# A token-major convolution on TensorE: from two 70x64 tiles of 192 columns to eight 39x32 tiles of 96 columns

## The chip, the cores and the metric

The kernel runs on one core of one Trainium2 chip. The metric is the device time of one execution in microseconds (us). Every ratio is between runs on the same chip in the same batch; traces are also compared across batches. Ratios use runs in the fast state alone; three runs, two of `start_after` and one of `best`, were more than 1.5% above the fastest of their kernel and are left out of them. The profile of a kernel is taken from one execution and shows a span some 1.8 us shorter than the time of the run.

Engines are named as the profile names them: PE is TensorE's matmuls, PEld its weight loads, DVE is VectorE, ACT ScalarE, POOL GpSimd, SP SyncE. L301 is line 301 of the kernel profiled, so the same statement has another number in another kernel.

## The reference, cut to what matters

```
# x: 8 x 4160 x 192 float32, weight: 8 heads x 7 taps
w   = softmax(weight, axis=-1)
y   = causal 7-tap convolution of x along the sequence, one set of taps per head of 24 channels
x2  = y.reshape(33280, 192)
h   = max(max(x2 @ w1, x2 @ w2), x2 @ w3)        # 192 -> 768
out = h @ w_out                                  # 768 -> 192, float32
```

## The kernel before

The 33280 tokens are worked on in 65 blocks of 512. The maximum is rewritten: max(y w1, y w2, y w3) = max(relu(y(w1-w3)), y(w2-w3)) + y w3, and the last term goes straight to the output through a small product M = w3 w_out. So per block TensorE does six groups of **layer one** (tiles `lp` and `lq`, one per half of the 128 rows, six matmuls of 512 columns in a group) and 60 matmuls of the **second layer** (tile `po`, 192 columns, in two halves of 30).

Layer one wants the convolved y with channels on partitions. Blocks 0 to 3 get it from a dense convolution (tile `D`). From block 4 on the convolution is token-major: x is loaded with tokens on partitions, GpSimd casts it to 16 bit, TensorE multiplies it by a band matrix of the taps (tile `G`), ScalarE and VectorE bring G to SBUF (tile `ys`), a DMA transposes it to channels on partitions, and two more DMAs **swap** the halves of the rows, so that each channel is there in both. Block 4 is done alone; blocks 5 and 6, 7 and 8, and so on in pairs, one convolution per pair: 30 pairs.

```
    def cast_x(t):                                   # GpSimd, 2 casts per block
        ...
        K = HALF + PAD                               # 64 + 6 rows
        for c in range(2):
            nc.gpsimd.tensor_copy(out=x16s[t0][0:K, :, c, u, :, :].rearrange("p h r c -> p r h c"),
                                  in_=xf[0:K, c:NR:2, :].rearrange("p r (h c) -> p r h c", c=GRP))
    ...
    def conv(t, pools):                              # 16 matmuls, 192 columns for a pair
        ...
        for h in range(NHEAD):
            for c in range(2):
                nc.tensor.matmul(
                    G[h // per][HALF * c:HALF * (c + 1), h % per, :],
                    lhsT=band[0:HALF + PAD, h, PAD:HALF + PAD],
                    rhs=x16s[t0][0:HALF + PAD, h, c, :, :, :].rearrange("p u r c -> p (u r c)"),
                    start=True, stop=True, tile_position=(0, HALF * c))
    ...
    def l1(t, j, pools=((psp, "p"), (psq, "q"))):    # one group of layer one
        ...
        for c in range(NC):
            for i in range(2):
                row = slice(HALF * i, HALF * (i + 1))
                nc.tensor.matmul(ps[i][:, 0:N], lhsT=wd[row, c, P * j:P * (j + 1)], rhs=y_all(t, i, c),
                                 start=(c == 0), stop=(c == NC - 1))
        r = rp.tile([P, NBLK], FP16, tag="r", name=f"r_{t}_{j}")
        nc.scalar.activation(out=r[:, 0:N], in_=ps[0][:, 0:N], func=AF.Relu)
        nc.vector.tensor_max(out=hs[t][:, j, 0:N], in0=r[:, 0:N], in1=ps[1][:, 0:N])
    ...
    for t in range(2, NB):                           # the main loop, cut
        ...                                          # loads of x, swaps, casts
        l1(t, 0)
        u = convs_at.get(t, t + 3 if t % 2 == 0 else NB)
        conv(u, PQ if t == 2 else WW + PQ)           # takes p and q buffers of layer one too
        ...                                          # evacuation of G, transposes
        st2(t - 1, 0, NJ)
        for j in range(1, NJ):
            l1(t, j)
            st2(t - 1, j, NJ)
        ...
```

The softmax here doesn't subtract the row's maximum and nothing guards it: scores larger than these inputs give would overflow.

## Time and profile before

| kernel before | |
|---|---|
| time, median of the runs with the changed kernel | 467.44 us (467.29 to 467.9) |
| span of the profile | 466.3 us |
| PE busy | 99% |
| one pair of blocks, from convolution to convolution | 13.74 us |
| of it TensorE held by the convolution | 0.87 us |
| last matmul starts | 462.39 us |

The prediction below shows the page of this profile: engines, chain and timeline. What it does not show is how close the two engines behind layer one are. These two lines are from the costliest groups: line, engine, operation, output and input, shapes, count, then busy time and the mean ns of one, then the idle time before it and what ended that.

```profile
L404 DVE TENSOR_TENSOR h<-r,lq 128x512 f16<-128x512 f16 x386 | 264.5, 685 | 98.6 <-ACT r L403 98.6
L403 ACT ACTIVATE r<-lp 128x512 f16<-128x512 f32 x386 | 230.5, 597 | 137.4 <-PE lp L399 123.9
```

A group of layer one is released only after ScalarE's 0.60 us and then VectorE's 0.69 us. There are two `q` buffers, so while that runs, TensorE must have other work. TensorE's timeline behind a convolution shows how it comes out; the columns are the start, the length and the piece of work.

```profile
209.34 0.38 PE L399 MATMUL lp<-yd,wd 64*128 64x512 f16 x1
209.44 0.37 PE L399 MATMUL lq<-yd,wd 64*128 64x512 f16 x1
209.55 0.38 PE L399 MATMUL lp<-yd,wd 64*128 64x512 f16 x1
```

`lq` starts 0.10 us behind `lp` and so keeps the beat of 0.21 us between two matmuls of one half. There is next to no room left in this place, and I did not see that when I predicted.

### The profile page before, as it was taken

How to read it: one execution, taken by the hardware profiler on the slowest of the kernel's cores; microseconds unless marked ns; L12 is line 12 of the kernel's file. 1: busy time of each engine (PE TensorE's matmuls, PEld its weight loads, DVE VectorE, ACT ScalarE, POOL GpSimd, SP SyncE). 2: the span in 40 equal slices, each digit the busy share in tenths (PEclk: the TensorE clock that was granted, in tenths of full speed). 3: DMA queues.
4: the chain of work that ended last, by engine and by line, in shares of the span. 5: the costliest groups of instructions: out<-in, count | busy, mean ns of one | idle time of the engine just before them, and what ended most of it. 6: DMA issues, size and time to landing. Idle time of an engine off the chain costs nothing.

```text
span 466.3 us, 17191 instructions
## 1 busy us (share of the span) xinstructions
PE 460.1 (99%) x7065; PEld 385.6 (83%) x7065; DVE 359.6 (77%) x607; ACT 317.0 (68%) x609; POOL 162.7 (35%) x227
## 2 busy tenths in 40 slices
PE   8899999999999999999999999999999999999996
PEld 4587888888888888889888888988888898888996
DVE  6787777777777777787877777777778777787775
ACT  5766767667666676676766667676676666766664
POOL 5664334234324324423423432432442343243010
PEclk9999999999999999999999999999999999999999
DMA  8958997778687777878777768767686976784512
GB/s 201 238 119 198 208 232 174 171 198 172 170 202 191 149 188 174 180 175 204 178 152 197 170 181 189 181 157 200 177 176 165 210 178 153 190 166 108 118 69 103
DMA packets 107114, 81.14 MB, mean 174 GB/s; under 512 B 53110, under 2 KB 101980, under 8 KB 107036
## 3 DMA queue, kind: packets, MB, share of 16 engines
q1 hardware_dynamic: 99804, 55.17, 57.6%
q0 software_dynamic: 7072, 24.78, 14.8%
q8 instruction: 55, 0.90, 0.9%
q14 instruction: 23, 0.19, 0.1%
q10 hardware_dynamic: 160, 0.10, 0.1%
HBM read 30.28 MB, written 25.56 MB: 120 GB/s over the span
## 4 chain that ended last, share of the span: by engine, by line
PE 95%; DMA 2%; SPq 2%; POOL 0%; issue 0%; DVE 0%; ACT 0%
PE lq L399 34%; PE po L442 33%; PE lp L399 22%; PE G L301 5%; DMA wos<-in_moe_w_out_dram 2%; SPq L190 1%; PE D L319 0%; SPq L134 0%; POOL wo L515 0%; PE pm L280 0%; PE pm L284 0%; DVE o L452 0%; ACT a L451 0%
## 5 line engine op out<-in xcount | busy, mean ns | idle before, releaser
L404 DVE TENSOR_TENSOR h<-r,lq 128x512 f16<-128x512 f16 x386 | 264.5, 685 | 98.6 <-ACT r L403 98.6
L403 ACT ACTIVATE r<-lp 128x512 f16<-128x512 f32 x386 | 230.5, 597 | 137.4 <-PE lp L399 123.9
L399 PE MATMUL lp<-yd,wd 64*128 64x512 f16 x1158 | 311.9, 376 | 1.3 <-DVE wd L256 1.3
L399 PE MATMUL lq<-yd,wd 64*128 64x512 f16 x1158 | 312.0, 376 | 0.0
L442 PE MATMUL po<-wo,h 64*128 64x192 f16 x3120 | 248.9, 243 | 0.0
L442 PEld LDWEIGHTS <-h 64*128 64x128 f16 x3120 | 203.6, 94 | 17.4
L399 PEld LDWEIGHTS <-wd 64*128 64x128 f16 x2340 | 166.6, 94 | 28.0 <-issue 3.4
L471 POOL DMA_DIRECT2D out_dram<-o x64 | 48.1, 752 | 281.4 <-DVE o L452 215.0
L158 POOL CAST x<-xf 70x768 f16<-70x768 f32 x122 | 97.4, 833 | 3.0 <-DMA xf<-in_x_dram 2.6
L442 PE MATMUL po<-m,yd 64*128 64x192 f16 x780 | 95.7, 243 | 0.0
L452 DVE TENSOR_TENSOR o<-a,po 128x384 f32<-128x384 f32 (+1 forms) x132 | 71.3, 542 | 0.6 <-ACT a L451 0.6
L442 PEld LDWEIGHTS <-yd 64*128 64x128 f16 x780 | 57.8, 94 | 10.8
L451 ACT COPY a<-po 128x384 f32<-128x384 f32 (+1 forms) x132 | 62.0, 471 | 2.1 <-PE po L442 2.1
L347 DVE CAST ys<-G 128x384 f16<-128x384 f32 x61 | 31.0, 550 | 0.0
L301 PEld LDWEIGHTS <-band 70*64 70x64 f16 x496 | 19.5, 109 | 12.8 <-PE lp L399 12.7
L347 ACT CAST ys<-G 128x384 f16<-128x384 f32 x61 | 26.2, 485 | 0.0
L301 PE MATMUL G<-x,band 70*64 70x192 f16 (+1 forms) x496 | 26.1, 248 | 0.0
L215 PE MATMUL idle<-idle 128*128 128x512 f16 x15 | 6.5, 581 | 1.2 <-DVE idle L210 1.2
L177 POOL CAST xz<-xf 112x80 f16<-112x80 f32 (+2 forms) x18 | 5.4, 340 | 3.9 <-DMA xf<-in_x_dram 3.0
L319 PEld LDWEIGHTS <-xz 112*32 112x32 f16 x240 | 4.7, 107 | 2.0 <-issue 1.3
L319 PE MATMUL D<-band,xz 112*32 112x103 f16 (+1 forms) x240 | 5.5, 229 | 0.0
L335 DVE COPY yd<-yd 64x512 f16<-64x512 f16 x9 | 4.3, 474 | 1.0 <-ACT yd L328 0.5
(45 smaller groups left out, 51.3 us busy)
## 6 DMA issues: line engine op xcount, KB each, us to landing
xf<-in_x_dram SPq DMA_DIRECT2D x57, 420.0 KB
out_dram<-o POOLq DMA_DIRECT2D x62, 384.0 KB, 3.8
yd<-yd SPq DMA_DIRECT2D x122, 96.0 KB
xf<-in_x_dram SPq DMA_DIRECT2D x7, 367.5 KB
ws<-in_moe_w_dram SPq DMA_DIRECT2D x6, 192.0 KB
yd<-ys SPq DMA_TRANSPOSE x61
w3s<-in_moe_w_dram SPq DMA_DIRECT2D x3, 192.0 KB
wos<-in_moe_w_out_dram SPq DMA_DIRECT2D x1, 576.0 KB
```

Source lines behind the costliest of these rows:

```text
L158: nc.gpsimd.tensor_copy(out=x16s[t0][0:K, :, c, u, :, :].rearrange("p h r c -> p r h c"), in_=xf[0:K, c:NR:2, :].rearrange("p r (h c) -> p ...
L215: nc.tensor.matmul(ps[:], lhsT=idle[:, 0:P], rhs=idle[:], start=True, stop=True)
L301: nc.tensor.matmul(G[h // per][HALF * c:HALF * (c + 1), h % per, :], lhsT=band[0:HALF + PAD, h, PAD:HALF + PAD], rhs=x16s[t0][0:HALF + PAD ...
L319: nc.tensor.matmul(ps[32 * g:32 * g + 32, lo:hi], lhsT=xz[t][v][0:rlen, q, 32 * s:32 * s + 32], rhs=band[0:rlen, h, cc:cc + hi - lo], star ...
L347: copy(out=slots[t][:, :, :, GRP * per * i:GRP * per * (i + 1)].rearrange("p u r (h c) -> p h (u r) c", c=GRP), in_=G[i][:].rearrange("p h ...
L399: nc.tensor.matmul(ps[i][:, 0:N], lhsT=wd[row, c, P * j:P * (j + 1)], rhs=y_all(t, i, c), start=(c == 0), stop=(c == NC - 1))
L403: nc.scalar.activation(out=r[:, 0:N], in_=ps[0][:, 0:N], func=AF.Relu)
L404: nc.vector.tensor_max(out=hs[t][:, j, 0:N], in0=r[:, 0:N], in1=ps[1][:, 0:N])
L442: nc.tensor.matmul(ps[b0, i][:, s % 2, :], lhsT=a, rhs=b, start=first, stop=last)
L451: nc.scalar.copy(out=a[:, ss, :], in_=ps[s0, 0][:, ss, :])
L452: nc.vector.tensor_add(out=outs[t][:, s0:s + 1, :], in0=a[:, ss, :], in1=ps[s0, 1][:, ss, :])
L471: qs[0].dma_start(out=bass.AP(tensor=out.tensor, offset=r * D, ap=[[D, n], [step * D, s1 - s0], [1, D]]), in_=ob[p0:p0 + n, s0:s1, :])
```

## The change

The intent: smaller tiles on TensorE. Instead of 16 matmuls of 192 columns in two tiles side by side, a pair's convolution is 64 matmuls of 96 columns in eight tiles: two row groups of 39 rows (32 tokens and 7 rows ahead of them) times four column groups of 32 tokens. The columns streamed, summed over a tile, fall by half. For this the loads split each block in two row groups, GpSimd casts in four pieces per block instead of two, and the DMA transposes and swaps are done once for a pair. Cut to its core:

```diff
-    NR = NBLK // HALF
+    TOK = 32
+    NR = NBLK // TOK // 2
+    LEAD = PAD + 1
+    KR = TOK + LEAD
 ...                                   (load_x: two row groups at partitions 0 and 64)
-        K = HALF + PAD
-        for c in range(2):
-            nc.gpsimd.tensor_copy(out=x16s[t0][0:K, :, c, u, :, :].rearrange("p h r c -> p r h c"),
-                                  in_=xf[0:K, c:NR:2, :].rearrange("p r (h c) -> p r h c", c=GRP))
+        for i in range(2):
+            row = slice(HALF * i, HALF * i + KR)
+            for r in range(2):
+                nc.gpsimd.tensor_copy(out=x16s[t0][row, :, :, u, r, :].rearrange("p h j c -> p j h c"),
+                                      in_=xf[row, 4 * r:4 * r + 4, :].rearrange("p j (h c) -> p j h c", c=GRP))
 ...
         for h in range(NHEAD):
-            for c in range(2):
-                nc.tensor.matmul(
-                    G[h // per][HALF * c:HALF * (c + 1), h % per, :],
-                    lhsT=band[0:HALF + PAD, h, PAD:HALF + PAD],
-                    rhs=x16s[t0][0:HALF + PAD, h, c, :, :, :].rearrange("p u r c -> p (u r c)"),
-                    start=True, stop=True, tile_position=(0, HALF * c))
+            for j in range(4):
+                for i in range(2):
+                    row = slice(HALF * i, HALF * i + KR)
+                    nc.tensor.matmul(
+                        G[2 * (h // per) + i][TOK * j:TOK * (j + 1), h % per, :],
+                        lhsT=band[row, h, HALF * i + LEAD:HALF * i + KR],
+                        rhs=x16s[t0][row, h, j, :, :, :].rearrange("p u r c -> p (u r c)"),
+                        start=True, stop=True, tile_position=(HALF * i, TOK * j))
 ...                                   (evacuation: same sizes, other places)
-        nc.sync.dma_start_transpose(out=yd[:, 0, :, :],
-                                    in_=slots[t0][:, u, :, :].rearrange("p r d -> p (r d)"))
+        for i in range(2):
+            nc.sync.dma_start_transpose(out=yp[:, 0, i, :, :, :].rearrange("p u k n -> p (u k) n"),
+                                        in_=slots[t][:, i, :, :, :].rearrange("p u r d -> p (u r d)"))
 ...
-                nc.sync.dma_start(out=yd[HALF * i:HALF * (i + 1), 1, :, :],
-                                  in_=yd[HALF * (1 - i):HALF * (2 - i), 0, :, :])
+                nc.sync.dma_start(out=yp[HALF * i:HALF * (i + 1), 1, :, :, :, :],
+                                  in_=yp[HALF * (1 - i):HALF * (2 - i), 0, :, :, :, :])
 ...
-    doubles_at = {2: (), 3: (4,), 4: (5, 6)}
+    doubles_at = {2: (), 3: (4,), 4: (5,)}
-        for u in doubles_at.get(t, (t + 2,)):
+        for u in doubles_at.get(t, (t + 2,) if t % 2 else ()):
```

More of the change, by code (lines that the diff above doesn't have):

```diff
@@ L87 @@
     NQ = len(chunks_of[0])
-    NR = NBLK // HALF
+    TOK = 32
+    NR = NBLK // TOK // 2
+    LEAD = PAD + 1
+    KR = TOK + LEAD
     def rows_of(t):
-        rows = [(b, S + o) for (b, S, N, off) in blocks[t] for o in range(0, N, HALF)]
-        assert len(rows) == NR
+        rows = [(b, S + o) for (b, S, N, off) in blocks[t] for o in range(0, N, TOK)]
+        assert len(rows) == 2 * NR
         return rows
@@ L100 @@
     ysp = ctx.enter_context(tc.tile_pool(name="ysp", bufs=3))
-    ydp = ctx.enter_context(tc.tile_pool(name="ydp", bufs=6))
+    ydp = ctx.enter_context(tc.tile_pool(name="ydp", bufs=4))
+    ypp = ctx.enter_context(tc.tile_pool(name="ypp", bufs=3))
     rp = ctx.enter_context(tc.tile_pool(name="rp", bufs=4))
@@ L118, in load_x @@
         if t < NDENSE:
-            todo = [(0, c[3], c[1] * SEQ + c[2]) for c in chunks_of[t]]
+            todo = [(0, c[3], c[1] * SEQ + c[2], i) for i, c in enumerate(chunks_of[t])]
         else:
-            todo = [(PAD, HALF, b * SEQ) if s == 0 else (0, HALF + PAD, b * SEQ + s - PAD)
-                    for b, s in rows_of(t)]
+            todo = [(HALF * (i // NR) + (0 if s else LEAD), KR if s else TOK,
+                     b * SEQ + s - (LEAD if s else 0), i % NR) for i, (b, s) in enumerate(rows_of(t))]
         parts = []
@@ L130, in load_x @@
             step = row[i + 1] - row[i] if k > i else 0
-            p0, rlen = todo[i][:2]
+            p0, rlen, _, q0 = todo[i]
+            q1 = todo[k][3] + 1
             src = bass.AP(tensor=x.tensor, offset=row[i] * D,
-                          ap=[[D, rlen], [step * D, k - i + 1], [1, D]])
-            eng.dma_start(out=xf[p0:p0 + rlen, i:k + 1, :], in_=src)
+                          ap=[[D, rlen], [step * D, q1 - q0], [1, D]])
+            eng.dma_start(out=xf[p0:p0 + rlen, q0:q1, :], in_=src)
             if parts and parts[-1][0] == rlen:
-                parts[-1] = (rlen, parts[-1][1], k + 1)
+                parts[-1] = (rlen, parts[-1][1], q1)
             else:
-                parts.append((rlen, i, k + 1))
+                parts.append((rlen, q0, q1))
             i = k + 1
@@ L152, in cast_x @@
         if u == 0:
-            x16s[t0] = x16p.tile([P, NHEAD, 2, nu, NR // 2, GRP], FP16, tag="x16", name=f"x16_{t0}")
+            x16s[t0] = x16p.tile([P, NHEAD, 4, nu, 2, GRP], FP16, tag="x16", name=f"x16_{t0}")
         if p0:
             nc.gpsimd.memset(xf[0:p0, 0, :], 0.0)
-        K = HALF + PAD
-        for c in range(2):
-            nc.gpsimd.tensor_copy(out=x16s[t0][0:K, :, c, u, :, :].rearrange("p h r c -> p r h c"),
-                                  in_=xf[0:K, c:NR:2, :].rearrange("p r (h c) -> p r h c", c=GRP))
+        for i in range(2):
[3 more added lines that the diff above has]
+                                      in_=xf[row, 4 * r:4 * r + 4, :].rearrange("p j (h c) -> p j h c", c=GRP))
     NC, NSLOT, CYC = D // HALF, D // 32, 96
-    NCH = NC * NBLK // P
     xz = {t: [const.tile([P, NQ, D], FP16, name=f"xz_{t}_{v}") for v in range(2)] for t in range(2)}
@@ L295, in conv @@
         n = len(pools)
-        per = NHEAD // n
-        w = nu * (NR // 2) * GRP
+        per = NHEAD * 2 // n
+        w = nu * 2 * GRP
         G = [pool.tile([P, per, w], FP32, tag=tag, name=f"G{i}_{t}") for i, (pool, tag) in enumerate(pools)]
         for h in range(NHEAD):
-            for c in range(2):
-                nc.tensor.matmul(
-                    G[h // per][HALF * c:HALF * (c + 1), h % per, :],
-                    lhsT=band[0:HALF + PAD, h, PAD:HALF + PAD],
-                    rhs=x16s[t0][0:HALF + PAD, h, c, :, :, :].rearrange("p u r c -> p (u r c)"),
-                    start=True, stop=True, tile_position=(0, HALF * c))
-        slots[t0] = ysp.tile([P, nu, NR // 2, D], FP16, tag="ys", name=f"ys_{t}")
+            for j in range(4):
[6 more added lines that the diff above has]
+                        start=True, stop=True, tile_position=(HALF * i, TOK * j))
+        slots[t0] = ysp.tile([P, 2, nu, 2, D], FP16, tag="ys", name=f"ys_{t}")
         convs[t0] = G
@@ L345, in evac @@
         G = convs[t]
-        per = NHEAD // len(G)
-        copy(out=slots[t][:, :, :, GRP * per * i:GRP * per * (i + 1)].rearrange(
+        per = NHEAD * 2 // len(G)
+        h0 = per * (i // 2)
+        copy(out=slots[t][:, i % 2, :, :, GRP * h0:GRP * (h0 + per)].rearrange(
                  "p u r (h c) -> p h (u r) c", c=GRP),
@@ L355, in turn, with spot @@
             return
-        t0, u, nu = place(t)
-        yd = dense[t] = ydp.tile([P, 2, NCH // 2, P], FP16, tag="yd", name=f"yd_{t}")
-        nc.sync.dma_start_transpose(out=yd[:, 0, :, :],
-                                    in_=slots[t0][:, u, :, :].rearrange("p r d -> p (r d)"))
+        nu = place(t)[2]
+        yp = ypp.tile([P, 2, 2, nu, NC, P], FP16, tag="yp", name=f"yp_{t}")
+        for u in range(nu):
+            dense[t + u] = yp
+        for i in range(2):
+            nc.sync.dma_start_transpose(out=yp[:, 0, i, :, :, :].rearrange("p u k n -> p (u k) n"),
+                                        in_=slots[t][:, i, :, :, :].rearrange("p u r d -> p (u r d)"))
     def double(t):
         if NDENSE <= t < NB:
-            yd = dense[t]
+            yp = dense[t]
             for i in range(2):
-                nc.sync.dma_start(out=yd[HALF * i:HALF * (i + 1), 1, :, :],
-                                  in_=yd[HALF * (1 - i):HALF * (2 - i), 0, :, :])
-    def spot(i, f):
-        return f // 2 + (0 if f % 2 == i else NCH // 2)
+                nc.sync.dma_start(out=yp[HALF * i:HALF * (i + 1), 1, :, :, :, :],
+                                  in_=yp[HALF * (1 - i):HALF * (2 - i), 0, :, :, :, :])
+    def spot(t, half, r, c):
+        _, u, nu = place(t)
+        f = NC * (r % 2) + c
+        return (((f % 2 != half) * 2 + r // 2) * nu + u) * NC + f // 2
     def y_all(t, i, c):
@@ L376, in y_all @@
             return dense[t][row, c, :]
-        a = dense[t][row, 0, 0, :]
-        s0, s1 = spot(i, c), spot(i, c + NC)
-        assert all(spot(i, NC * r + c) == (s1 if r % 2 else s0) + NC * (r // 2) for r in range(4))
-        return bass.AP(tensor=a.tensor, offset=a.offset + P * s0,
-                       ap=[list(a.ap[0]), [P * NC, 2], [P * (s1 - s0), 2], [1, P]])
+        a = dense[t][row, 0, 0, 0, 0, :]
+        k = [spot(t, i, r, c) for r in range(4)]
+        assert k[1] - k[0] == k[3] - k[2]
+        return bass.AP(tensor=a.tensor, offset=a.offset + P * k[0],
+                       ap=[list(a.ap[0]), [P * (k[2] - k[0]), 2], [P * (k[1] - k[0]), 2], [1, P]])
     def y_tok(t, i, c, s):
@@ L386, in y_tok @@
             return dense[t][row, c, P * s:P * (s + 1)]
-        k = spot(i, NC * s + c)
-        return dense[t][row, k // (NCH // 2), k % (NCH // 2), :]
+        a = dense[t][row, 0, 0, 0, 0, :]
+        return bass.AP(tensor=a.tensor, offset=a.offset + P * spot(t, i, s, c), ap=[list(a.ap[0]), [1, P]])
     def l1(t, j, pools=((psp, "p"), (psq, "q"))):
@@ L566 @@
             turn(5)
-            turn(6)
             load_x(9)
@@ L570 @@
             cast_x(8)
-        else:
+        elif t % 2 == 0:
             turn(t + 3)
```

## The prediction

> **What bounds the kernel now.** I read the page first: its table of engines, then the chain that ended last, then the costliest groups.
>
> ```profile
> span 466.3 us, 17191 instructions
> ...
> PE 460.1 (99%) x7065; PEld 385.6 (83%) x7065; DVE 359.6 (77%) x607; ACT 317.0 (68%) x609; POOL 162.7 (35%) x227
> ...
> PE 95%; DMA 2%; SPq 2%; POOL 0%; issue 0%; DVE 0%; ACT 0%
> PE lq L399 34%; PE po L442 33%; PE lp L399 22%; PE G L301 5%; DMA wos<-in_moe_w_out_dram 2%; SPq L190 1%; PE D L319 0%; SPq L134 0%; POOL wo L515 0%; PE pm L280 0%; PE pm L284 0%; DVE o L452 0%; ACT a L451 0%
> ```
>
> TensorE is the bound: 95% of the chain is its matmuls, nothing waits on another engine for long, and the granted clock is full. The part that the change touches is G, the token-major convolution, 5.1% in the chain. A microsecond taken from G shortens the run by one, as long as its inputs are there and its outputs are taken away in time. I then read the timeline of TensorE round one convolution and round two others of a different shape:
>
> ```profile
> 207.83 0.38 PE L399 MATMUL lq<-yd,wd 64*128 64x512 f16 x1
> 208.13 0.85 PE L301 MATMUL G<-x,band 70*64 70x192 f16 x16
> 208.92 0.34 PE L442 MATMUL po<-m,yd 64*128 64x192 f16 x3
> ```
> ```profile
> 23.16 1.10 PE L319 MATMUL D<-band,xz 112*32 112x103 f16 x60
> ...
> 28.83 0.53 PE L301 MATMUL G<-x,band 70*64 70x96 f16 x16
> ```
>
> The first column is the start, the second the length of the merged piece. The layer-one matmul at 207.83 streams 512 columns; such matmuls on one half of the rows follow each other every 0.216 us in this trace, so its slot ends at 208.04. The next stage starts at 208.92. **One convolution of a pair thus holds TensorE for 0.87 us**, and it does so 30 times (480 matmuls of 192 columns, 16 each): 26 us. Of the 0.87 us, (0.85 - 0.25)/15 = 40 ns per matmul is streaming, two side by side in 82 ns, eight rounds: 0.66 us. The remaining 0.21 us is change-over: 0.09 us from 208.04 to 208.13 ahead, 0.10 us behind (last start 208.74 by the trace, plus 82 ns, to 208.92), and some 0.02 us in which the second round waits for weights.
>
> [...]
> - [...] 0.09 and 0.10 us are lost on the two sides of each G. The new shape is still another mode than the 64x128 of its neighbours, so both stay.
> - [...] In this trace the two tiles of a G round start 3 to 4 ns apart. Four tiles work at full pace: D is 60 matmuls, 40 in four column tiles and 20 in two. At 45 ns a round that is 10 + 10 rounds = 0.91 us; the piece has 1.10 - 0.21 = 0.89 us from first start to last. No run here shows eight.
> - [...]
> - [...] VectorE's h, o and ys each read at most one operand from SBUF, the other from PSUM, and the trace has their durations the same beside a GpSimd cast (h 685 ns) as without. Doubling GpSimd's work should not slow VectorE.
>
> **The change part by part.**
> 1. *Convolution matmuls.* Removed: 16 of 192 columns in two tiles. Added: 8 heads x 4 x 2 = 64 of 96 columns in eight tiles. A 96-column round takes 43 ns by this trace (block 4's G: (0.53 - 0.21)/15 = 21 ns, two side by side). 64/8 = 8 rounds x 43 = 0.34 us, plus some 0.02 us for the first weights and 0.03 us for the last of eight starts; change-over 0.19 us as now. Sum **0.58 us against 0.87: 0.29 us less, x30 = 8.7 us**, all on the path. Condition: 16 instructions (8 weight loads, 8 matmuls) must be issued in each 43 ns. In D, 8 came in bursts of 13 to 17 ns, under 2 ns each, so 16 need some 30 ns. It fits, with little room.
> 2. *Block 4 alone*: 64 matmuls of 48 columns for 16 of 96; pure streaming falls from 0.34 to 0.18 us, likely bound by issue. Under 0.2 us: left out.
> 3. *GpSimd casts.* Twice as many, each still 768 elements per partition:
>
> ```profile
> L158 POOL CAST x<-xf 70x768 f16<-70x768 f32 x122 | 97.4, 833 | 3.0 <-DMA xf<-in_x_dram 2.6
> ```
>
>    I take 833 ns each, as the length per partition is the same and fewer partitions should not help; back to back they come every 0.78 us (four in 3.13 us). So +122 x 0.8 = 97 us of GpSimd work, 35% to 56%. In the steady part it is hidden, but narrowly:
>
> ```profile
> 202.72 0.75 POOL L471 DMA_DIRECT2D out_dram<-o  x1 [5.00 <-DVE o L452]
> 203.47 0.25 POOL L155 MEMSET xf<- 6x192 f32 x1
> 203.78 1.59 POOL L158 CAST x<-xf 70x768 f16<-70x768 f32 x2
> ```
>
>    These casts are the second block of the pair whose convolution starts at 208.13. Four end at 203.78 + 3.14 = 206.9, 1.2 us ahead. At the start it does not fit:
>
> ```profile
> 29.90 3.13 POOL L158 CAST x<-xf 70x768 f16<-70x768 f32 x4
> 36.89 0.76 POOL L471 DMA_DIRECT2D out_dram<-o  x1 [3.87 <-DVE o L452]
> 37.65 1.60 POOL L158 CAST x<-xf 70x768 f16<-70x768 f32 x2
> 39.18 0.25 POOL L155 MEMSET xf<- 6x192 f32 x1
> 39.49 1.58 POOL L158 CAST x<-xf 70x768 f16<-70x768 f32 x2
> ```
>
>    Blocks 5 and 6 are cast from 29.90; eight casts end at 36.2, and the convolution that needs them is at 35.85: 0.3 us of waiting. Blocks 7 and 8 follow from 37.65; with the memset they end at 44.2, and their convolution is at 43.27: 0.9 us. After that GpSimd has caught up. Together with block 4, whose casts end near 28.9 and are needed at 28.83, **1.2 us lost, once**.
> 4. *Loads of x*: 78 rows x 8 for 70 x 8 per block, 11% more bytes, two issues for one. A block's load is issued more than a block before its cast in the steady part. Hidden.
> 5. *Transposes and swaps*: the same bytes; the swaps go in half as many transfers of twice the run, the queue's program falls from 209 rows to 156. They are finished more than one block (6.4 us) before layer one reads them, now and then. Off the path: worth nothing.
> 6. *Evacuation of G*: still four of 128x384 per pair, same engines. ScalarE's and VectorE's next needs at the layer-one pools leave some 0.4 us after TensorE comes back 0.3 us earlier. Nothing.
>
> Sum: 467.5 - 8.7 + 1.2 = 460.0; with a little for imperfect packing, **460.3 us** (-1.5%).
>
> **The rivals.**
> - *Issue becomes the bound.* Eight tiles need 2.7 ns per instruction over 128 instructions; the densest sustained stretch here is D's, 5.7 ns, though that was limited by columns. For: nobody has shown eight here, and in D the fourth tile often started 8 to 10 ns behind the third. Against: the bursts. At 5.7 ns the convolution would take 0.73 + 0.19 = 0.92 us, more than now, and the run some 470 us; a middle, 55 to 60 ns a round, gives 462 to 463 us.
> - *GpSimd becomes the wait in each pair.* If the casts took over 1.1 us each instead of 0.8, or came late, every convolution would wait. For: the room is 1.2 us of 6.4. Against: the fixed 833 ns. At 1.2 us each it would take back some 0.5 us x 30 and the gain would be gone: about 467 us.
> - *The full gain without the loss at the start*: if the early casts are in time, because the stretch before has time to give, 458.5 us, just short of 2%. If the change-over is shorter too[...], some 3 us more: 456 us.
> - *DMA contention in the saturated stretch*, 35 to 49 us, where the mean DMA share is 0.91: more load bytes may make layer one wait once, 1 us.
>
> **Range and chances.** The steady gain lies between 6 us (imperfect rounds) and 10 us (perfect, nothing else), the loss at the start between 0 and 2.5 us. That gives 457 to 464.5 us for 8 in 10. Faster by over 2% means under 458.2 us: it needs nearly perfect packing and hardly a loss at the start, or a cheaper change-over: 0.2. Slower by over 2% needs the issue limit and GpSimd at once: 0.03. Within 2%: 0.77.
>
> **What would show it right or wrong.** In the profile after: TensorE still 95% of the chain; the piece of 64 G matmuls with 0.35 to 0.4 us from first start to last and 0.56 to 0.62 us of hold; the interval between two pairs' convolutions 0.3 us shorter than the present 13.74 us; casts of 39x768 at about 833 ns and GpSimd near 56%; waits of TensorE for GpSimd's x16 of about 1 us in all, before 45 us only. A piece of G near 0.7 us would show the issue rival; waits for x16 in every pair the GpSimd rival; the same hold but a longer period would be a wait I have not seen. What would make the prediction wrong most likely is the pace of eight tiles, which no trace here shows.

## The result, and the profile after

| | before | after |
|---|---|---|
| median (lowest to highest), us | 467.44 (467.29 to 467.9) | 473.22 (472.32 to 476.03) |
| ratio after/before, 95% interval | | 1.0132 (1.0088 to 1.0176) |
| span of the profile, us | 466.3 | 471.0 |

A ratio is the mean time of one kernel's fast runs over the mean of the other's fast runs of the same rounds, so it is not quite the ratio of the medians. The changed kernel is 1.3% slower: within 2%, but outside the predicted range, on the far side of zero. A second batch (`after_again`, below) gave 472.63 us.

First the page of the changed kernel: span, engines, the granted clock in 40 slices of the span, the chain that ended last by engine, and the queue that brings instructions (packets, MB, share). The same queue line of the kernel before is in the fence behind it.

```profile
span 471.0 us, 20214 instructions
PE 461.0 (98%) x8553; PEld 360.4 (77%) x8553; DVE 359.9 (76%) x607; ACT 323.2 (69%) x609; POOL 260.7 (55%) x349
PEclk9999899999999999999999999999999999999999
q8 instruction: 67, 1.10, 1.1%
PE 95%; DMA 2%; DVE 1%; issue 1%; ACT 0%; DVEq 0%; SPq 0%
```
```profile
q8 instruction: 55, 0.90, 0.9%
```

TensorE is still the bound, at 95% of the chain. Three things differ from the page before. A slice of the clock is below 9. VectorE and "issue" have 1% each in the chain. And TensorE's program has grown by 2976 instructions (1488 matmuls and as many weight loads), so 67 packets of 16 KB bring instructions instead of 55.

Now the piece itself. These lines are TensorE's timeline round a convolution of the changed kernel, at the same place as the one before in the prediction:

```profile
212.15 0.38 PE L413 MATMUL lq<-yp,wd 64*128 64x512 f16 x1
212.46 0.74 PE L308 MATMUL G<-x,band 39*32 39x96 f16 x64
213.13 0.34 PE L456 MATMUL po<-m,yp 64*128 64x192 f16 x3
...
213.55 0.38 PE L413 MATMUL lp<-yp,wd 64*128 64x512 f16 x1
213.74 0.37 PE L413 MATMUL lq<-yp,wd 64*128 64x512 f16 x1
213.77 0.38 PE L413 MATMUL lp<-yp,wd 64*128 64x512 f16 x1
```

From `lq` to `po` it is 0.975 us, of which 0.216 us are lq's own slot: the convolution holds TensorE for **0.76 us, where 0.58 was predicted and 0.87 was measured before**. And behind it `lq` starts 0.19 us after `lp`, not 0.10: some of what was saved is lost again at once.

I split TensorE's time between convolutions in the two traces into the *hold* (from the start of the last layer-one matmul ahead of the convolution to the next matmul behind it) and the *rest* (up to the last layer-one matmul ahead of the next convolution):

| us | before | after | difference |
|---|---|---|---|
| start of the hold of blocks 9/10, the fourth convolution | 56.66 | 61.37 | +4.71 |
| hold, each pair | 1.089 | 0.975 | -0.114 |
| rest, each pair (mean, undisturbed) | 12.650 | 12.706 | +0.056 |
| stalls after 61 us (one of 0.87, four of 0.09) | 0 | 1.2 | +1.2 |
| last matmul | 462.39 | 466.75 | +4.36 |

The sum checks: 4.71 + 27 x (-0.114 + 0.056) + 1.2 = 4.34, against 4.36 measured. So three questions are open: why the hold shrank by 0.11 and not by 0.29; what takes 0.056 us per pair back; and where 4.7 us at the start and the stalls come from.

**The start.** The 4.71 us are made up like this (intervals between convolutions, after minus before): up to block 4's convolution +0.29; in it +0.14; blocks 5/6's convolution +0.45; the stretch behind it +2.27; the next convolution -0.12; the stretch behind that +1.68. The two timelines of TensorE in the changed kernel show what these are:

```profile
36.28 0.21 PE L308 MATMUL G<-x,band 39*32 39x96 f16 x1
36.85 0.72 PE L308 MATMUL G<-x,band 39*32 39x96 f16 x63 [0.36 <-POOL x L164]
```
```profile
45.56 0.37 PE L413 MATMUL lp<-yp,wd 64*128 64x512 f16 x1 [2.07 <-DMA yp<-yp]
...
47.59 0.63 PE L413 MATMUL lp<-yp,wd 64*128 64x512 f16 x1
48.01 0.63 PE L413 MATMUL lp<-yp,wd 64*128 64x512 f16 x1
```

At 36.85 the convolution waits 0.36 us for a GpSimd cast: that was predicted. At 45.56 layer one of block 4 waits 2.07 us for the *swap* of its rows: that was not. After this pause the granted clock is 0.50 from 47.4 to 50.8 us, for 3.4 us, against 1.00 on both sides of that stretch, and a matmul takes 0.63 us instead of 0.38. The length of a pause alone does not decide this here: 2.11 us at the same place in `short_h` and 1.69 us in `best` (both below) brought no half clock (mean granted clock 1.000 in both profiles, 0.996 here).

The chain of waits in this stretch, and the issuing queue (start, length, piece), show how the swap came to be late:

```profile
34.27 4.92 DMA yp<-ys
39.24 6.19 DMA yp<-yp
```
```profile
35.55 3.08 SPq L139 DMA_DIRECT2D xf<-in_x_dram  x3
39.24 1.14 SPq L377 DMA_DIRECT2D yp<-yp  x2
```

The transpose of block 4 (`yp<-ys`) takes 4.92 us beside other transfers. Three loads of x go out between, and the swap (`yp<-yp`) then takes 6.19 us. Before, the same queue showed two loads and an earlier swap:

```profile
33.47 1.21 SPq L134 DMA_DIRECT2D xf<-in_x_dram  x2
...
38.03 1.14 SPq L366 DMA_DIRECT2D yd<-yd  x2
```

The two halves of the swap were issued at 38.03 and 38.57 us and had landed by 40.76 and 41.03 us, 1.5 us ahead of their use. At the start the transfers are not "more than one block" ahead, as the prediction had it.

**A stall later on.** TensorE's timeline at the largest stall after 61 us:

```profile
267.19 0.74 PE L308 MATMUL G<-x,band 39*32 39x96 f16 x64
267.85 0.34 PE L456 MATMUL po<-m,yp 64*128 64x192 f16 x3
267.95 0.24 PE L456 MATMUL po<-wo,h 64*128 64x192 f16 x1
268.99 0.42 PE L456 MATMUL po<-wo,h 64*128 64x192 f16 x6 [0.79 <-issue]
```

"issue" means that nothing in the profile was waited for. It starts shortly after a convolution.

### The profile page after: what moved, and what is told of

Same layout as the page of the kernel before. It is cut to its first block, busy times and chain, and to the rows that moved or that the text cites. A ratio compares the mean times of both kernels' runs of the same rounds, so it can differ in the third digit from the quotient of the medians.

```text
span 471.0 us, 20214 instructions
## 1 busy us (share of the span) xinstructions
PE 461.0 (98%) x8553; PEld 360.4 (77%) x8553; DVE 359.9 (76%) x607; ACT 323.2 (69%) x609; POOL 260.7 (55%) x349
## 4 chain that ended last, share of the span: by engine, by line
PE 95%; DMA 2%; DVE 1%; issue 1%; ACT 0%; DVEq 0%; SPq 0%
PE lq L413 38%; PE po L456 35%; PE lp L413 14%; PE G L308 4%; PE idle L220 1%; DMA yp<-yp 1%; DMA yp<-ys 1%; PE D L326 1%; PE lw L413 0%; DVE wd L261 0%; DVE o L466 0%; DVE yd L342 0%; PE band_cols L244 0%; DVE h L418 0%; DVE yd L333 0%
## 5 line engine op out<-in xcount | busy, mean ns | idle before, releaser
L413 PE MATMUL lp<-yp,wd 64*128 64x512 f16 x1098 | 297.1, 377 | 2.1 <-DMA yp<-yp 2.1
L413 PE MATMUL lq<-yp,wd 64*128 64x512 f16 x1098 | 296.6, 377 | 0.0
L456 PE MATMUL po<-wo,h 64*128 64x192 f16 x3120 | 266.0, 243 | 0.8 <-issue 0.8
L164 POOL CAST x<-xf 39x768 f16<-39x768 f32 x244 | 195.1, 827 | 9.5 <-PE lq L413 2.8
L456 PE MATMUL po<-m,yp 64*128 64x192 f16 x732 | 101.4, 243 | 0.0
L456 PEld LDWEIGHTS <-yp 64*128 64x128 f16 x732 | 56.1, 94 | 10.3
L308 PEld LDWEIGHTS <-band 39*32 39x32 f16 x1984 | 18.7, 91 | 13.6 <-PE lp L413 12.7
L308 PE MATMUL G<-x,band 39*32 39x96 f16 (+1 forms) x1984 | 23.0, 207 | 0.4 <-POOL x L164 0.4
L413 PE MATMUL lp<-yd,wd 64*128 64x512 f16 x60 | 16.2, 377 | 1.3 <-DVE wd L261 1.3
L413 PE MATMUL lq<-yd,wd 64*128 64x512 f16 x60 | 16.4, 376 | 0.0
```

Source lines behind the costliest of these rows:

```text
L164: nc.gpsimd.tensor_copy(out=x16s[t0][row, :, :, u, r, :].rearrange("p h j c -> p j h c"), in_=xf[row, 4 * r:4 * r + 4, :].rearrange("p j ( ...
L308: nc.tensor.matmul(G[2 * (h // per) + i][TOK * j:TOK * (j + 1), h % per, :], lhsT=band[row, h, HALF * i + LEAD:HALF * i + KR], rhs=x16s[t0 ...
L456: nc.tensor.matmul(ps[b0, i][:, s % 2, :], lhsT=a, rhs=b, start=first, stop=last)
```

## The experiments

I had these theories. **The queue**: weight loads and matmuls can't be issued as fast for a whole convolution as for a few rounds. **The wait moved** (A in the texts on record): the 0.056 us per pair is layer one's second group waiting for its PSUM buffer. **The start**: transfers and casts before 60 us collide. **The instruction blocks** (D in the texts on record): the longer program makes TensorE wait for its own instructions. The texts on record use letters; what each stands for there is plain from the words beside it. All results are right unless said.

### 1. The pace of eight tiles: `pace`

The changed kernel, with seven bursts of matmuls added at its very end, each between a few matmuls of full width; not timed against anything, only looked at.

```diff
+    def burst(name, count, n, tiles, k=KR):
+        keep_warm(3)
+        ps = [psw.tile([P, NBLK], FP32, tag="w", name=f"{name}_{i}") for i in range(2)]
+        for e in range(count):
+            z = e % tiles
+            i, j = (z % 2, z // 2) if tiles == 8 else (0, z)
+            row = slice(HALF * i, HALF * i + k)
+            nc.tensor.matmul(ps[i][TOK * j:TOK * (j + 1), 0:n], lhsT=band[row, e // 8 % NHEAD, LEAD:KR],
+                             rhs=idle[row, 0:n], start=True, stop=True, tile_position=(HALF * i, TOK * j))
+    burst("bea", 64, 96, 8)    # as the kernel's own
+    burst("beb", 64, 48, 8)    # half the columns
+    burst("bec", 64, 192, 8)   # twice the columns
+    burst("bed", 64, 48, 4)
+    burst("bee", 64, 96, 4)
+    burst("bef", 32, 96, 8)
+    burst("beg", 128, 96, 8)   # twice as many
```

> The changed kernel with bursts of matmuls at its end, outputs untouched: 64 in eight tiles at 96, 48 and 192 columns, 64 in four column tiles at 48 and 96 columns, 32 and 128 in eight tiles at 96 columns. Theory C (after the 32 pairs of weight load and matmul[...], TensorE gets one instruction every 4.2 ns, 8.4 ns a pair): the first 32 of each burst run at the pace of their columns (42 ns a round of eight at 96), the rest at 8.4 ns each, 67 ns a round, at 48 and at 96 columns and in four tiles at 48 columns (34 ns a round of four) too; at 192 columns and in four tiles at 96 (43 ns a round) columns decide throughout; 32 alone never slow down. Rival (eight tiles share something, weights or PSUM, so that a round takes 67 ns): 32 alone are slow too or the slow part begins elsewhere, and four tiles at 48 columns run at their columns' pace, 23 ns a round.

Measured: the starts of every eighth matmul, in ns from the first of its burst. All have 64 matmuls but `beg`, which has 128 and of which the first eleven rounds are given. A stroke is where the burst was broken by a stall for instructions.

| burst | tiles, columns | starts of rounds of eight |
|---|---|---|
| bea | 8, 96 | 0, 53, 96, 138, **240**, 307, 373, 440 |
| beb | 8, 48 | 0, 40, 66, 93, **221** / 588, 627, 658 |
| bec | 8, 192 | 0, 93, 176, 258, 341, 423, 506, 588 |
| bee | 4, 96 | 85 for each eight, to the end |
| beg | 8, 96 | 0, 54, 96, 139, **241**, 307, 374, 441, 507, 574, 641, ... |

The same numbers stand in the kernel's own convolutions. Block 4's has 48 columns and goes 26 to 27 ns a round for four rounds, then 67. On the timeline of the changed kernel its 64 matmuls take nearly as long as those of twice the columns:

```profile
29.12 0.67 PE L308 MATMUL G<-x,band 39*32 39x48 f16 x64
```

The first 32 matmuls go at the pace of the columns: 42 to 43 ns a round, which is what was predicted. The 33rd starts only 0.22 to 0.24 us after the first, and from there on it is **67 ns a round, whether 96 or 48 columns**: 8.4 ns for each weight load with its matmul. With 192 columns (83 ns a round) or four tiles (85 ns) the columns are the slower of the two, and no break is seen. 32 matmuls with their weight loads are 64 instructions, and 8.4 ns a pair is 4.2 ns an instruction. What inside TensorE puts the break there is not shown by any run. Bursts `bed` (four tiles, 48 columns) and `bef` (32 matmuls) were broken by stalls (1.14 and 0.76 us of "issue"), so whether 32 alone never slow down stayed untested. But `bed` settles the rival in the text on record, that it is something which eight tiles share:

```profile
469.94 0.35 PE L606 MATMUL bed<-idle,band 39*32 39x48 f16 x27
471.43 0.45 PE L606 MATMUL bed<-idle,band 39*32 39x48 f16 x37 [1.14 <-issue]
```

Of the 37 matmuls behind the stall, the first 32 go at 25 ns for four, and the last five start 8 to 9 ns apart. So four tiles show the slow pace too, again after 32, and the count began anew with the stall.

So the hold is made up as follows: 0.306 us ahead of the first matmul (0.216 of them lq's slot, 0.09 change-over), 0.525 from the first start to the last, 0.145 behind. The prediction had 0.35 to 0.4 us from the first start to the last at most. Its pace of 42 to 43 ns would have made seven rounds 0.30 us; with the late 33rd matmul and the slow rounds the eighth began at 0.44.

### 2. The wait behind the convolution: `order_after`, `order_before`

After the change there is less work between the first and the second group of layer one of the block in which the convolution is done: 0.65 + 0.76 + 0.41 = 1.82 us (first group, convolution, second-layer matmuls). Before it was 0.65 + 0.87 + 0.41 = 1.93 us. ScalarE, VectorE and the release need some 2.04 us by the trace. If that is the wait, six more second-layer matmuls ahead of the second group should remove it.

```diff
-        for e in range(n * u // NU, n * (u + 1) // NU):
+        def cut(v):
+            if first is None or v == 0:
+                return n * v // NU
+            return first + (n - first) * (v - 1) // (NU - 1)
+        for e in range(cut(u), cut(u + 1)):
 ...
+        first = 8 if t > 2 and t % 2 == 0 and t + 3 < NB else None      # 7 in order_before
-        st2(t - 1, 0, NJ)
+        st2(t - 1, 0, NJ, first)
```

> The changed kernel, with one thing moved: in the iterations that hold a convolution, 16 of the 60 second-layer matmuls (instead of 10) stand between the convolution and the next layer-one group, the other five groups share the rest. Theory A (the gain of the shorter convolution is given back to a wait: layer one's second group needs the q bank that VectorE's max of the first group frees, some 1.4 us after the first group, whatever the convolution takes): the stretch between two convolutions falls from 12.71 us to about 12.53 us, 27 pairs x 0.17 = 4 to 5 us less, 468 to 469 us. Rival (the extra 0.06 us of that stretch is GpSimd, DMA or instruction supply): no change, within 1 us of 473 us.

> The kernel before, with the same move (14 of 60 matmuls ahead of the second group). Theory A: the stretch falls from 12.61 and 12.69 us (in turn) to about 12.53 us, 28 x 0.12 = 3 to 3.5 us less: about 464 us. Rival: no change, 467.5 us.

Measured: `order_after` 475.28 us (474.16 to 476.35), ratio 1.0151 (1.0114 to 1.0187). `order_before` 468.76 us (468.41 to 469.75), ratio 1.0008 (0.9979 to 1.0037). In the profiles the rest per pair did not fall: 12.77 us for `order_after` (12.706 without the edit), 12.69 for `order_before` (mean 12.65 without). The second group started on time, but the wait, 0.26 us, now stood at the fourth group.

What follows: the theory in its first form fell. The matmuls put ahead were missing later, and the chain ScalarE to VectorE to TensorE was as tight there. This does not say that the wait is not of this chain, only that it can't be moved away.

### 3. The wait measured by shortening its cause: `short_h`

The first group of the block with the convolution works on 128 of its 512 columns, so that ScalarE and VectorE are done sooner. **The result is wrong on purpose** (relative error 0.27).

```diff
+        if j == 0 and t >= 4 and t % 2 == 0 and t + 3 < NB:
+            N = P
+            nc.gpsimd.memset(hs[t][:, j, N:NBLK], 0.0)
         nc.scalar.activation(out=r[:, 0:N], in_=ps[0][:, 0:N], func=AF.Relu)
         nc.vector.tensor_max(out=hs[t][:, j, 0:N], in0=r[:, 0:N], in1=ps[1][:, 0:N])
```

> Wrong result on purpose: the changed kernel, but in the 29 iterations that hold a convolution of blocks 7 and up the first layer-one group evacuates 128 of its 512 columns (ScalarE and VectorE each some 0.4 to 0.5 us shorter; GpSimd zeroes the rest). TensorE's work is the same. Theory A in its sharper form (the earlier move only pushed the wait two groups on; the ring of two p/q buffers needs some 2.04 us from one group to the next user of its buffer, and the convolution sits in that ring): with the first group's buffer free 0.9 us sooner the 0.19 us wait goes, the stretch between convolutions falls from 12.71 to about 12.52 us, 27 x 0.19 = 5 us less than the changed kernel. Rival (the bubble of 0.19 us is TensorE's own, a change-over or instruction supply): the stretch stays at 12.71 us.

Measured: 470.44 us (469.96 to 471.39), ratio 1.0057 (1.0042 to 1.0072). The rest per pair fell from 12.706 to **12.650 us**, 0.056 us less, and not the 0.19 less that I had put down for it. TensorE's timeline behind the convolution, to be held against that of the changed kernel above (213.13 to 213.77):

```profile
213.12 0.37 PE L459 MATMUL po<-m,yp 64*128 64x192 f16 x3
...
213.59 0.38 PE L413 MATMUL lp<-yp,wd 64*128 64x512 f16 x1
213.65 0.38 PE L413 MATMUL lq<-yp,wd 64*128 64x512 f16 x1
213.80 0.38 PE L413 MATMUL lp<-yp,wd 64*128 64x512 f16 x1
```

`lq` is 0.06 us behind `lp` instead of 0.19. What follows: this lag of `lq` is a wait for the q buffer, which is freed once ScalarE and VectorE are done with the first group (the edit shortens both, so it does not tell them apart). The traces show what a lag costs: it is carried on from group to group (in `order_after` partly as a later `lp`), and the next convolution waits for the half that is behind. The rest less the largest lag is 12.51 us in four kernels: 12.611 - 0.100 and 12.689 - 0.177 in turn before the change, 12.706 - 0.193 after it, 12.773 - 0.260 in `order_after`, 12.690 - 0.177 in `order_before`. So the lag was there before, and the shorter convolution raised its mean from 0.138 to 0.193 us: that is the give-back. In `short_h` the later groups keep a lag of 0.10 us, and `lp` of the second group comes 0.04 us later than in the changed kernel, which no run explains; that the net fall equals the give-back is chance. The total time of this run is not used for it, as its start differs.

### 4. The start: `start_after`, `loads_only`

Both move loads of x ahead of other transfers; `start_after` also makes the early casts sooner.

```diff
 # loads_only
-            cross_dma(3)
-            load_x(7)
+            load_x(7)
+            load_x(8)
+            cross_dma(3)
 ...
-            turn(4)
-            load_x(8)
+            turn(4)
 # start_after: the same, and
+    cast_x(5)
     store(0, 0, 4, (nc.gpsimd,))
 ...
-            cast_x(5)
             cast_x(6)
+            cast_x(7)
 ...
-            cast_x(7)
             cast_x(8)
```

> The changed kernel, start only: the loads of blocks 7 and 8 are issued ahead of the swaps of block 3 instead of ahead of and behind the transposes of block 4, and the casts of blocks 5 and 7 stand ahead of the stores of blocks 0 and 1. Theory B (4.4 us of the loss are one chain at the start: casts late for the convolution of blocks 5 and 6, block 4's swap stuck behind the larger loads of block 8, TensorE idle 2 us and then at half clock for 3.4 us): the convolution of blocks 9 and 10 comes at about 57 us instead of 61.4, and the run is 4 to 4.5 us shorter, about 469 us; no half clock near 47 us. Rival (the late swap comes from the swaps' and transposes' own new form, per pair and in halves): block 4 still waits 2 us, under 1 us gained.

> The changed kernel, of the repair of the start only the loads of blocks 7 and 8 moved ahead of the swaps of block 3; casts as they were. If the loads that stand ahead of block 4's swap cost the 2 us and the half clock after it, these go, and what stays is the wait for the casts, 0.4 us at the first pair and about 1 us at the second: the fourth convolution at 58 to 59 us instead of 61.4, about 470.5 us plus whatever stalls come. If the casts are the larger part, it gains under 1 us.

Measured: `start_after` 472.28 us (468.7 to 478.21), ratio 1.005 (1.0006 to 1.0093); `loads_only` 470.21 us (468.55 to 472.54), ratio 1.0042 (1.0005 to 1.0079). The fourth convolution's hold began at 59.10 and 58.15 us, against 61.37 in the first profile of the changed kernel.

The early cast in `start_after` has a cost of its own. VectorE's copies across partitions of block 2 now all run beside GpSimd's casts. These are VectorE's timelines, of `start_after` and of the changed kernel:

```profile
26.45 2.64 DVE L342 COPY yd<-yd 64x512 f16<-64x512 f16 x3
```
```profile
25.15 2.17 DVE L342 COPY yd<-yd 64x512 f16<-64x512 f16 x3
```

Three copies take 2.64 us here, 2.17 in the changed kernel (1.94 before); one takes 0.28 to 0.29 us where GpSimd is quiet and 0.80 to 0.94 beside its casts of x16. The prediction looked only at VectorE's PSUM-reading instructions (before the change h takes 685 ns without a cast beside it and 687 with one), and left out the copies from SBUF to SBUF at the start. TensorE's block 4 convolution came at 30.89 us, 1.8 us later than in the changed kernel; the copies account for 0.47 of it, as they had already begun 1.3 us later.

What follows: putting the loads first takes away layer one's wait for block 4's swap. In the six profiles without the move that wait is 2.07 us (changed kernel), 2.05 (`order_after`), 2.11 (`short_h`), 0.80 (`pace`), 0.85 (`shift_after`, where the profile names a load of x) and none (`after_again`); in the five with it it is at most 0.09 us. That the kernel as a whole gains by it is not shown: `after_again`, without an edit, has its fourth convolution at 58.16 us too, and the interval of its ratio overlaps that of `loads_only`. The fast runs of `start_after` still lie between 468.7 and 472.91 us (the two others, at 478, are left out, which flatters its ratio if they belong to the same spread at the start). The eleven runs of the kernel before in that batch lie between 467.33 and 472.13, nine of them within 1.3 us. The start is not under control with this.

### 5. The same kernel again: `after_again`

No edit.

> The changed kernel itself, for more executions and a second profile beside the others on one chip. If the spread is chance of instruction blocks and of the start: 471 to 477 us again, the profile with its stalls at 193 modulo 256, in other pairs than the first time, and with the start's chain (block 4's swap, half clock) again. If these belonged to the one profiled execution, they are not there.

Measured: 472.63 us (469.42 to 475.06), ratio 1.010 (1.0065 to 1.0136); the fourth convolution at 58.16 us in its profile, not 61.37. So 3.2 of the 4.7 us at the start of the first profile were not there in another execution of the same kernel. There TensorE waited 0.36 and 0.71 us for casts, and not for block 4's swap. Stalls of TensorE labelled "issue" were there at 59.56 to 60.05 and 128.18 to 129.01 us. What follows: the loss at the start and the stalls vary between executions; the hold and the rest do not. One profile must not be taken for the mean.

### 6. The instruction blocks: `shift_after`, `shift_loads`, `shift_start2`

All the larger stalls after 60 us have two things in common in the traces. They stand at the same place in TensorE's program, an instruction number of about 193 modulo 256 (counted over the matmuls, weight loads and semaphore instructions of TensorE's queue). And they end 1.2 to 1.6 us after a packet of the instruction queue has landed: the packet at 265.86 to 267.43 us, the stall's end at 268.99. A packet of 16 KB is 256 instructions (67 packets for some 17140 instructions; in the steady part TensorE starts 255.7 of them from one packet to the next on average, and 256.0 in the kernel before). In the changed kernel the 128 instructions of a convolution always lie inside one such block, just ahead of this boundary (they begin at 42 to 69 modulo 256), so that block lasts only some 5.1 us where the blocks before lasted 8.3. The margin from a packet's landing to its need falls: at least 3.9 us before, at least 1.3 us after.

If so, putting the boundary *inside* a convolution, so that each of two blocks gets half of it, should remove the stalls. 37 tiny matmuls in the warm-up move all that follows by 74 instructions.

```diff
     keep_warm(6, psp, "p")
+    small = psp.tile([P, NBLK], FP32, tag="p", name="small")
+    for _ in range(37):
+        nc.tensor.matmul(small[:, 0:8], lhsT=idle[:, 0:P], rhs=idle[:, 0:8], start=True, stop=True)
 # shift_loads: this and loads_only
 # shift_start2: this and start_after, with cast_x(5) held back until block 2's copies are done:
+    after_cross = const.tile([P, 2], FP16)
+    nc.gpsimd.tensor_copy(out=after_cross[:], in_=dense[2][:, 1, 0:2])
     cast_x(5)
```

> The changed kernel with 37 tiny matmuls (74 instructions, under 1 us, while TensorE waits for the first loads anyway) at its start, nothing else. Theory D (the sporadic stalls of 0.4 to 1 us behind a convolution, always at the same place modulo 256 in TensorE's instruction order, are a wait for the next block of 256 instructions; the convolution's 128 are used up in 0.75 us, and all of them lie in one block, so that block lasts 5.1 us instead of 8.3): the shift lets the block boundary fall into the middle of each convolution, both blocks of a pair last some 6.8 us, no stall after 50 us, runs within 1 us of each other, about 471.5 us. Rival (the stalls and the spread come from late swaps, loads or casts): the spread of the changed kernel stays, 472 to 476 us or more.

> Both: the 37 tiny matmuls and the moved loads. Theories B and D together: no stalls, no idle TensorE before 50 us beyond 1.5 us for the casts: 468.5 to 469.5 us, spread under 1 us. If D is wrong: spread of several us.

> As shift_loads, and the casts of blocks 5 and 7 ahead of the stores of blocks 0 and 1 as in the earlier run, but behind VectorE's copies of block 2 (a tiny GpSimd copy that reads their result holds the casts back), since in the earlier run these copies took 0.88 us each beside the casts instead of 0.47 and cost 1.2 us. All of the start's loss gone but the slower first convolution: the fourth convolution near 57 us, 466.5 to 467.5 us, the same as before within 1 us, spread under 1 us.

Measured:

| | us (lowest to highest) | ratio | fourth convolution, us | stalls of 0.3 us or more after 60 us |
|---|---|---|---|---|
| shift_after | 472.34 (469.56 to 475.46) | 1.009 (1.0046 to 1.0135) | 60.21 | none |
| shift_loads | 469.56 (468.32 to 473.05) | 1.0025 (0.999 to 1.006) | 63.22 | none |
| shift_start2 | 470.77 (468.22 to 474.5) | 1.0054 (1.0014 to 1.0095) | 61.00 | none |

The place at which the changed kernel had its stall at 267.95, in `shift_after`, as TensorE's timeline has it:

```profile
265.74 0.74 PE L311 MATMUL G<-x,band 39*32 39x96 f16 x64
266.41 0.34 PE L459 MATMUL po<-m,yp 64*128 64x192 f16 x3
266.52 0.49 PE L459 MATMUL po<-wo,h 64*128 64x192 f16 x7
```

No stall. In all five profiles with the boundary in a convolution (these three and the two kernels of 7 and 8) there was none after 60 us; of the seven profiled executions with the old boundary (the changed kernel, `after_again`, `order_after`, `start_after`, `short_h`, `pace`, `loads_only`) six had at least one, and `loads_only` had none. The kernel before and `order_before` had none. The smallest margin in those five is 2.2 us. So the theory holds for the later part. It does not explain the spread between runs, which stayed at 4.7 to 6.3 us, and moving a boundary can hit another dense stretch. In `shift_start2` it fell into the dense convolution of block 3:

```profile
28.54 0.59 PE L329 MATMUL D<-band,xz 112*32 112x103 f16 x35
30.95 0.68 PE L329 MATMUL D<-band,xz 112*32 112x100 f16 x25 [1.82 <-issue]
```

1.82 us of "issue", and the half clock from 31.6 to 35 us behind it. `shift_loads` shows the half clock too, from 18.6 to 22 us. So the fourth convolution of the shifted kernels comes no sooner, and `shift_start2`, expected at 466.5 to 467.5 us, is a miss. Its held-back cast did not help the copies either: they took 2.61 us, now beside block 4's own casts.

### 7. All repairs together: `best`

`start_after` with the held-back cast, and the shift made only at block 7's convolution, by 37 matmuls of 4 columns, so that the dense convolutions keep their boundaries.

```diff
+        for e in range(37 if t == 7 else 0):
+            i, j = e % 2, e // 2 % 4
+            row = slice(HALF * i, HALF * i + KR)
+            nc.tensor.matmul(G[i][TOK * j:TOK * (j + 1), 0, 0:4],
+                             lhsT=band[row, 0, HALF * i + LEAD:HALF * i + KR],
+                             rhs=x16s[t0][row, 0, j, 0, 0, 0:4],
+                             start=True, stop=True, tile_position=(HALF * i, TOK * j))
```

> Correct, meant to be the best of the changed kind: loads of blocks 7 and 8 early, casts of blocks 5 and 7 ahead of the stores but behind VectorE's copies, and the 37 tiny matmuls not at the start, where they moved a block boundary into the dense convolution (1.8 us of waiting, then half clock), but at the convolution of blocks 7 and 8 (0.3 to 0.5 us once). No stall after 60 us, fourth convolution at 57 to 57.5 us, 466.5 us, spread under 2 us. If the start still meets waits that depend on chance: 467 to 471 us.

Measured: 471.23 us (469.55 to 477.51, the last of them left out of the ratio), ratio 1.0068 (1.0054 to 1.0082). A miss. The chain of waits up to 62 us names what was left of it:

```profile
35.23 1.69 issue
...
43.20 3.57 DMA yp<-ys
...
47.35 6.93 DMA yp<-yp
```

A stall for instructions at 35.2 us, before the shift has been made, and a pair's swap of 6.93 us. I did not mend the new path at the start with these moves; whether others would is open.

### 8. The old path at the start, the new one afterwards: `hybrid`

Blocks 4 to 12 are loaded, cast, convolved, transposed and swapped as before; blocks 13 to 64 as in the change. 20 tiny matmuls at the convolution of blocks 13/14 put the block boundary into the convolutions. Cut to its core:

```diff
+    SWITCH = 13
+    def old(t):
+        return NDENSE <= t < SWITCH
 ...                       (in load_x, cast_x, conv, evac, turn, double, y_all, y_tok:)
+        if old(t):
+            conv_old(t, pools)          # the body of the kernel before
+            return
 ...
+        for e in range(20 if t == SWITCH else 0):    # tiny matmuls as in 7
```

> Correct, meant to beat both: blocks 4 to 12 are loaded, cast, convolved, transposed and swapped as in the kernel before, blocks 13 to 64 as in the changed kernel, with 20 tiny matmuls at the convolution of blocks 13 and 14 so that the block boundary of TensorE's instructions falls into the middle of the later convolutions. If the start's loss and the stalls are all that stands against the new convolution, the start is that of the kernel before (fourth convolution near 56.7 us), 26 pairs gain 0.115 us at the convolution less 0.056 us of waiting, 1.5 us, minus 0.2 us for the tiny matmuls: 466.2 us, 0.3% faster than before, runs within 1 us. If something else of the new form costs time later ([...]pair-wise swaps), it is not faster, or spreads.

Measured: **466.01 us** (465.76 to 468.23), ratio 0.9956 (0.9926 to 0.9986): faster than the kernel before by 0.4%, on the same chip and in the same rounds (467.76 us, 467.39 to 470.9). In its profile the holds after the switch are 0.975 us, the rest 12.705 us, and there is no stall after 60 us:

```profile
427.98 0.38 PE L515 MATMUL lq<-yp,wd 64*128 64x512 f16 x1
428.29 0.74 PE L359 MATMUL G<-x,band 39*32 39x96 f16 x64
428.96 0.33 PE L558 MATMUL po<-m,yp 64*128 64x192 f16 x3
```

By the table of the two traces 26 pairs x 0.058 us make 1.5 us; the medians differ by 1.75. Two of its six runs, 467.88 and 468.23 us, are no faster than the median before, so the runs are not within 1 us as expected. The profile is of the slower of the two: its fourth hold began at 58.35 us, not at 56.66, and the loss lies ahead of the first token-major convolution, whose hold began at 29.19 us instead of 27.34. From the start of the fourth hold to the last matmul it took 404.36 us against 405.73 before, 1.37 us less. What follows: the change is worth some 0.06 us per pair in the steady part, as long as the start and the supply of instructions are left alone. As it mends both at once, it does not tell which of the two is worth more.

## Why the prediction was wrong

- **Part 1, the convolution (0.58 us against 0.87): wrong, and the first failing step.** The change-over was right: 0.09 us ahead, 0.145 behind including the last matmul's own streaming. The 43 ns a round held for four rounds. "In D, 8 came in bursts of 13 to 17 ns, under 2 ns each, so 16 need some 30 ns. It fits" took the pace of a short burst for one that lasts. Experiment 1 measured 67 ns a round for the other 32 matmuls, which began only 0.24 us after the first. The term was 0.29 us per pair and measured 0.114. The issue rival named it, with 55 to 60 ns a round and 462 to 463 us; it was worse, and it was given too little.
- **Part 2, block 4: wrong by its conclusion.** "Under 0.2 us: left out"; it took 0.67 us for 48 columns, 0.14 us *more* than before.
- **Part 3, the casts: right.** 827 ns against 833 predicted, GpSimd 55% against 56%, no wait for x16 in the steady part. The wait at the start was 0.36 us for blocks 5/6 in the profile, not 1.2 us in all: later ones lay behind the wait for the swap. In `after_again` and `loads_only`, where that swap was in time, the casts cost 0.36 + 0.71 and 0.34 + 0.76 us, near the 1.2.
- **Part 4 and 5, loads, transposes and swaps: right in the steady part, wrong at the start, and the second failing step.** "They are finished more than one block before layer one reads them" was read from the steady part. Block 4's swap had 1.5 us to spare before, and in the profile it became a wait of 2.07 us, and a half clock of 3.4 us behind it. The rival of contention at 35 to 49 us, put at 1 us, had the right place and was sized at a quarter: the start lost 4.7 us in one execution and 1.5 in another (58.16 against 56.66).
- **Part 6, "leave some 0.4 us ... Nothing": wrong.** Layer one was waiting for its q buffer already, and the shorter convolution gave 0.056 us of 0.114 back in each pair. Experiment 3 and the lags in the traces show it.
- **Left out altogether: the supply of instructions.** 2976 more instructions look free in the table of engines. They come in blocks of 256 (16 KB a packet), and the densest stretch of the program set the margin. Experiment 6 shows it after 60 us: with the boundary inside the convolution none of five profiles had a stall there, with the old one six of seven did.
- **Sums that do not come out.** 55 to 60 ns a round instead of 43 add 2.9 to 4.1 us: 463 to 464.5 us, not 462 to 463. Waits of 0.5 us in 30 pairs are 15 us: the GpSimd rival is some 475 us, not 467. Without the loss at the start it is 458.8, not 458.5. And the queue's program does not shrink: SyncE issued 272 transfers before and 280 after. None of these decided the outcome.
- **How the 12.9 us between 460.3 and 473.22 divide,** an estimate from the two profiles: 5.3 from the pace (30 x 0.176), 1.6 from the give-back, 3.5 at the start (4.7 less the 1.2 foreseen), 1.2 from stalls; the other 1.3 lie between these two executions and the medians.
- **What stays open.** How the loss at the start is shared among the late swap, the casts, the half clock and the instruction stalls, over executions: each is shown in some profile, and they replace each other. Why the start varies by 2 to 6 us from run to run in the kernels that have the new path there, where most runs of the kernel before lie within 1 us (with single ones at 469.8 to 472.1). And what happens inside TensorE's queue at the 65th instruction.

## What to carry to other kernels

Splitting a matmul into smaller tiles buys columns and pays in instructions: before you do it, count the weight loads and matmuls against a *sustained* pace (here 8.4 ns a pair, once 64 instructions have gone by), not against a burst. Where a stretch of the program becomes dense in instructions, look where it lies in the blocks in which they arrive (here 256 instructions each). And read the start of a kernel for itself: a margin from the steady part says nothing of it, and the version that won was the one that left the start as it was.
